# Holding back sixteen DRAM stores in an FFT convolution, and sharing out the evictions behind it

## The chip, the cores and the metric

The kernel runs on one core of a Trainium2 chip. The metric is the device time of one execution, in microseconds. A core has five engines that run beside each other, each through its own instruction stream in order: TensorE (PE in the profile; its weight loads are listed as PEld), VectorE (DVE), ScalarE (ACT), GpSimd (POOL) and SyncE (SP). In this kernel nearly every DMA is issued by SP, so SP's stream is the queue of the transfers: an issue that has to wait holds up all the issues behind it.

## What is computed

Four layers on an array x of 2048 positions by 512 features: local attention, long convolution, local attention, long convolution, each on a layernorm of x and added to it.

```python
x = A_x
x = x + _A_ref(_layernorm(x, axis=-1), A_wqkv, A_wo)
x = x + _B_ref(_layernorm(x, axis=-1), B_A_re, B_A_im, B_B_re, B_B_im, B_C_re, B_C_im, B_log_dt, B_Dskip)
x = x + _A_ref(_layernorm(x, axis=-1), A_wqkv, A_wo)
x = x + _B_ref(_layernorm(x, axis=-1), B_A_re, B_A_im, B_B_re, B_B_im, B_C_re, B_C_im, B_log_dt, B_Dskip)
```

The change lies in the first `_B_ref` (and at the border to the second attention). With the transforms cut to what matters:

```python
K = jnp.einsum("dn,dnl,dn->dl", Cc, P, dB).real      # one convolution kernel per feature
Kf = rfft2(pad(K)); Uf = rfft2(pad(u))
Yf = Uf * Kf
y = irfft2(Yf)[..., :L] + u * Dskip
```

The spectrum Kf is the same in both convolution layers. The first convolution computes it, uses it, and writes it to DRAM; the second reads it back.

## The kernel before

Class `FftB` is one convolution layer; `tag` is 0 for the first and 1 for the second. The features are in two groups (g = 0, 1), and the length-4096 transform is done in two steps of matmuls each way. The order of the work is written out by hand, as a string of tokens that `run` (line 829) walks through; each engine then executes its share in that order. For the first convolution the string is `ORDER0`, and then `ORDERF`, which also carries the beginning of the second attention layer. The tokens:

- `K`, `U`: first transform step of the convolution kernel and of the input (`f1`, line 711): PE, then an eviction from PSUM by DVE (`D`) or ACT (`A`) into the tile a1s.
- `k`: second step of the convolution kernel (`k_f2`, line 730). One token gives one *piece* of the spectrum, 128 partitions by 1024 values of bf16 (256 KB); there are 16 pieces, k0 to k15. The piece is evicted (line 709) into a slot taken from the list `self.free`.
- `u`: second step of the input (`u_f2`, line 776), evicted by ACT into one of three `ub` buffers (line 782).
- `m`: the product of piece n with the input's spectrum (`u_mult`, line 764): two DVE instructions (line 769), the first with the piece itself, `kn`, the second with `ks`, the same piece with each pair of neighbouring partitions exchanged (the other part of a complex product). They add to the tiles t1 and t2 of the group.
- `y`: first step back (`i1`, line 784), y0 to y7 from the t tiles of group 0, y8 to y15 from those of group 1. So y8 can only start when the last product, m15, is done. 32 matmuls and one eviction each.
- `z`: last step back (`i2`, line 801), which adds to x_sb; `z01D` is group 0, row block 1, by DVE.
- In `ORDERF`, `h`, `a`, `p`, `n`, `T`, `E`, `P`, `Q` are the layernorm statistics, the transposes and the K and Q projections of the second attention layer.

The exchanged copy `ks` is made by two DMAs per piece (`kf_load`, line 750, issues at line 755), SBUF to SBUF, 64 partitions (128 KB) each. Here they are called the *exchange* of piece n. `pump` (line 745) issues the exchanges up to four ahead of the products, or further while slots are plentiful; it is called after each `k` and each `m`. After each product the piece is stored to DRAM by one DMA of 256 KB (line 772, the *store* of piece n), and both slots go back to the list. The store only reads `kn`, so it does not wait for the product itself.

Slots: twelve at first, three in the part of the tile w_sb that w2 leaves over (here w0, w1, w2), six in kn tiles (kn0a to kn2b), three in kf_sb (wk0 to wk2); eight more (kf_nat) when the last `K` token is done. In the profile they go by those tile names. Before the change the exchanges and stores around the middle of the stage stand on SP in this order (target <- source):

```
store 0 (w0) | exchange 4 (w0<-kn2b) | store 1 (w2) | exchange 5 (w1<-wk0) | store 2 (kn0b) |
exchange 6 (w2<-wk1) | store 3 (kn1b) | exchange 7 (kn0a<-wk2) | store 4 | exchange 8 (kn1a<-kn0b) |
exchange 9 (kn2a<-kn1b) | store 5 | exchanges 10, 11, 12 | store 6 | exchange 13 | exchange 14 |
store 7 | exchange 15 (w1<-wk0) | stores 8 to 15 | weights of the second attention layer
```

PSUM: `ptile` (line 704) deals out four buffers in turn, so a tile of PSUM is written again four tiles later. In `ORDERF` the last five tiles of group 0 (y3 to y7) are evicted by ACT, y8 by ACT, y9 by DVE, y10 to y12 by ACT, then z01 by DVE, y13 by DVE, y14 and y15 by ACT.

The weights of the second attention layer are loaded by `front_w` (line 226): two DMAs of 512 KB into the tile kT_ext, the half for K first (line 227), the half for Q (line 228). That tile lies over memory that w_sb and the kn tiles held before, so these DMAs wait for the stores that read it. `front_k` (line 255) is the first to use it.

Of the kernel before, what the change touches and what calls it, by code (L numbers as in the profile page):

```python
# [21 lines left out]
S = 2048  # L22
# [15 lines left out]
NG = 2  # L38
DQG = 64
EC = 16  # L40
NEC = 128 // EC
# [12 lines left out]
"""  # L54
LATE0 = "a s t g r b m"
ORDERF = """
yA yA yA yA yA yA yD yA yA yA z01D yD yA yA z00A z10A z11A h01 h00 h10 a0 z12A
p0 h11 z02A n0 a1 z03A h02 S T0 p1 E01D n1 E00A h12 a2 z13A P02 P01 h03 T1
E10A Q00 E11D p2 P03 P00 n2 h13 P10 P12 a3 T2 E21D E20A p3 n3 P11 P13 P23 P21
T3 E31D x1 E30A P20 P22  # L60
"""
ORDER1 = """
UD UA UD UA UD UA UD UA UD UA UD u UD u u m UA u m UD UA m u m u m
# [112 lines left out]
class LayerA:  # L176


    def __init__(self, tc, nc, consts, lnst, A_wqkv, A_wo, layer, xnT, nq):
        self.tc, self.nc, self.c, self.lnst, self.layer = tc, nc, consts, lnst, layer  # L180
        self.ctx = ExitStack()
        self.keep = self.ctx.enter_context(tc.tile_pool(name=f"a{layer}_keep", bufs=1, side="right"))
        slot = self.keep.tile([P, NDT * (2 * D + (NA + 14) * P)], BF16, name="kT_ext", tag="slot")
        self.wqk = slot[:, 0:NDT * 2 * D].rearrange("p (t c) -> p t c", t=NDT)
        self.wsrc = A_wqkv.rearrange("(dt p) c -> p dt c", p=P)
        self.A_wo = A_wo
        self.kT = slot[:, NDT * 2 * D:].rearrange("p (t a q) -> p t a q", t=NDT, q=P)
        self.xnT = xnT
        self.qT = {q: self.q_tile(q) for q in range(nq)}
        self.ps_l = self.wv = None  # L190
        self.xns = {}
        self.st = [dict() for _ in range(4)]
# [477 lines left out]
class FftB:  # L670


    def __init__(self, tc, nc, C, ident, w2_dram, g2_dram, kf_dram, x_sb, tag):
        self.tc, self.nc, self.C, self.ident, self.kf_dram, self.x_sb = tc, nc, C, ident, kf_dram, x_sb
        self.w2_dram, self.g2_dram = w2_dram, g2_dram
        self.tag = tag
        self.c_grp, self.c_mid, self.c_ps = ExitStack(), ExitStack(), ExitStack()
        self.grp = self.c_grp.enter_context(tc.tile_pool(name=f"b{tag}_grp", bufs=5, reuse_waits="tile"))
        self.ps = [c.enter_context(tc.tile_pool(name=f"b{tag}_ps_{side}", bufs=2, space=PSUM, side=side))
                   for c, side in ((self.c_ps, "right"), (self.c_grp, "left"))]  # L680
        self.npt = 0
        self.kf, self.nat, self.ub, self.cnt = {}, {}, {}, {}
        self.nkf = 0
        g2p = self.c_grp.enter_context(tc.tile_pool(name=f"b{tag}_g2", bufs=1, reuse_waits="tile"))
        self.g2 = g2p.tile([P, 2, 16, P], BF16, name="g2_sb")
        self.S = [dict() for _ in range(NG)]
# [43 lines left out]
    def k_f2(self, g, ec, eng):  # L730
        n = g * NEC + ec
        p2 = self.f2(g, "ka", ec)
        kf = self.nat[n] = self.free.pop(0)
        self.evac(kf, p2, eng)
        self.nk += 1
        self.pump()
# [13 lines left out]
    def kf_load(self, n):  # L750
        sync, (g, ec) = self.nc.sync, divmod(n, NEC)
        if self.tag == 0:
            kn, ks = self.nat[n], self.free.pop(0)
            for h in range(2):
                sync.dma_start(ks[h::2], kn[1 - h::2])
            self.kf[n] = kn, ks
            return
        kc = self.ring[n % len(self.ring)]
        sync.dma_start(kc[0::2], self.kf_dram[g, ec])
        for r in range(2):  # L760
            sync.dma_start(kc[1::2, r], self.kf_dram[g, ec, :, 1 - r])
        self.kf[n] = kc[:, 0], kc[:, 1]

    def u_mult(self, g, ec):
        n = g * NEC + ec
        kn, ks = self.kf.pop(n)
        ub = self.ub.pop(n)
        for t, k in zip(self.S[g]["t"], (kn, ks)):
            self.nc.vector.tensor_tensor(t[:, :, ec * EC:(ec + 1) * EC], ub[:], k, ALU.mult)  # L769
        self.nm += 1  # L770
        if self.tag == 0:
            self.nc.sync.dma_start(self.kf_dram[g, ec].rearrange("p r q e -> (p r) (q e)"), kn.rearrange("p q e -> p (q e)"))
            self.free += [kn, ks]
        self.pump()

    def u_f2(self, g, ec):
        nc = self.nc
        if ec == 0:
            self.S[g]["t"] = tuple(self.gtile(n, [P, DQG, P]) for n in ("t1", "t2"))
        p2 = self.f2(g, "ua", ec)  # L780
        ub = self.ub[g * NEC + ec] = self.wk.tile([P, DQG, EC], BF16, name="ub")
        nc.scalar.copy(ub[:], p2)  # L782
# [660 lines left out]
```

## Time and profile before

| | us |
|---|---|
| median of 3 runs | 420.19 (419.57 to 420.63) |
| the profiled execution, as timed | 420.44 |
| its span in the trace | 418.6 |
| DVE busy | 387.1 (92% of the span) |
| ACT busy | 323.0 (77%) |
| PE busy | 321.3 (77%) |
| stores of pieces (line 772) | 16 issues of 256 KB, 3.3 median from issue to landing |
| exchanges (line 755) | 32 issues of 128 KB, 3.4 median to landing |

The profiled execution took 420.44 us, 1.84 more than its span; that is what lies before the first and after the last instruction of the trace. The mean granted clock of TensorE was 0.981 of full speed. The first convolution runs from about 195 us of the span to about 262 us; the products m0 to m15 lie between 213.77 and 243.90.

In the lines of an engine's order of time, the first number is the start in us from the span's start, the second the duration, then engine, source line, operation and tiles (out<-in); in brackets at the end stands how long the engine had been idle, and what released it. "SPq" is SP issuing a DMA. In lines by window the columns are the window and its length, busy time of PE, PEld, DVE, ACT and POOL with the number of instructions in brackets, granted clock, busy share of the DMA engines, and GB/s.

### The profile page before, as it was taken

To read this page: it belongs to the slowest core of one execution; us is meant where nothing else is said; L and a number is where in the kernel's file an instruction comes from. 1 tells how busy PE (TensorE), PEld (TensorE's weight loads), DVE (VectorE), ACT (ScalarE), POOL (GpSimd) and SP (SyncE) were. 2 spreads that over 40 slices of the span, in tenths; PEclk is the share of its full clock that TensorE was granted. 3 is DMA by queue.
4 is the path that set the end of the run, shared out by engine and by line. 5 is a ranking of instruction groups with operands and counts; after the bars stand their busy time and mean duration, and the time that the engine had idled before them with its cause. 6 is when DMAs were issued, how large, how long until landed. Compare 5 with 4: busy or idle time off the path is not lost.

```text
span 418.6 us, 15862 instructions
## 1 busy us (share of the span) xinstructions
PE 321.3 (77%) x7046; PEld 232.5 (56%) x7104; DVE 387.1 (92%) x515; ACT 323.0 (77%) x554; POOL 37.7 (9%) x46
## 2 busy tenths in 40 slices
PE   3000068999999987888998779999998978896785
PEld 2000036667756555556887668556555656666664
DVE  8999999999899999997999949979779999989995
ACT  5999998986445569997999978874555657889972
POOL 3000200000396000001400000000000020000000
PEclk9999998999999999999999969999999998999999
DMA  7940642123015666393245597730043018504506
GB/s 205 390 132 13 73 90 70 33 45 84 15 39 136 171 173 189 85 397 114 78 146 199 187 307 207 208 121 2 2 115 89 3 56 351 155 3 131 176 7 199
DMA packets 62462, 54.36 MB, mean 130 GB/s; under 512 B 33877, under 2 KB 50874, under 8 KB 61114
## 3 DMA queue, kind: packets, MB, share of 16 engines
q1 hardware_dynamic: 62250, 53.22, 42.1%
q8 instruction: 55, 0.90, 0.9%
q10 hardware_dynamic: 144, 0.13, 0.1%
q14 instruction: 13, 0.11, 0.1%
HBM read 30.28 MB, written 13.24 MB: 104 GB/s over the span
## 4 chain that ended last, share of the span: by engine, by line
PE 38%; DVE 24%; ACT 9%; DMA 7%; issue 6%; SPq 1%; DVEq 0%; ACTq 0%
DVE pav L413 8%; PE pq L359 6%; DVE a1s L709 4%; PE L L315 4%; DVE t L769 4%; PE pk L1139 4%; PE po L428 4%; PE pq L439 3%; PE pq L198 3%; DVE prod L308 3%; PE pp L255 3%; PE pp L1077 3%; DMA w_sb<-w_dram 2%; PE pb L796 2%; PE pb L821 1%
## 5 line engine op out<-in xcount | busy, mean ns | idle before, releaser
L413 DVE TENSOR_TENSOR pav<-attn,v_ext 128x4096 bf16<-128x4096 bf16 (+1 forms) x34 | 72.9, 2158 | 0.2 <-PE pq L439 0.2
L308 DVE TENSOR_TENSOR prod<-qT,kT_ext 128x4096 bf16<-128x4096 bf16 x29 | 66.0, 2300 | 3.9 <-PE L L315 3.8
L428 PE MATMUL po<-ident,pav 64*128 64x64 bf16 x2048 | 36.7, 192 | 14.2 <-DVE pav L413 8.1
L428 PEld LDWEIGHTS <-pav 64*128 64x128 bf16 x2048 | 33.2, 96 | 25.0 <-DVE pav L413 15.6
L1067 PE MATMUL pt<-ident,x_blk 128*128 128x128 bf16 x64 | 7.0, 260 | 43.4 <-ACT x_blk L171 43.4
L979 DVE TENSOR_TENSOR A_t<-A_t,pow_t 128x1024 bf16<-128x1024 bf16 (+4 forms) x46 | 38.1, 870 | 0.2
L439 PE MATMUL pq<-wop,oT 128*128 128x512 bf16 x121 | 31.6, 380 | 4.0 <-issue 3.6
L782 ACT CAST ub<-pb 128x1024 bf16<-128x1024 f32 x32 | 32.2, 1035 | 1.8 <-DVE t L769 0.8
L361 ACT CAST v_ext<-pq 128x512 bf16<-128x512 f32 x32 | 18.8, 587 | 19.2 <-PE pq L359 17.5
L727 PE MATMUL pb<-a1s,w_sb 128*128 128x64 bf16 x768 | 27.2, 193 | 6.4 <-ACT a1s L709 2.9
L315 PEld LDWEIGHTS <-prod 128*128 128x128 bf16 x928 | 27.0, 96 | 8.1 <-DVE prod L308 2.5
L1067 PEld LDWEIGHTS <-x_blk 128*128 128x128 bf16 x64 | 5.4, 117 | 46.1 <-ACT x_blk L171 44.3
L359 PE MATMUL pq<-wv,xnT 128*128 128x512 bf16 x118 | 29.9, 379 | 0.5
L709 DVE CAST a1s<-pb 128x1024 bf16<-128x1024 f32 x23 | 27.0, 1216 | 3.4 <-PE pb L720 3.4
L1077 PE MATMUL pp<-xnT,kT_ext 128*128 128x512 bf16 x87 | 24.9, 404 | 6.4 <-ACT qT L1082 3.4
L727 PEld LDWEIGHTS <-w_sb 128*128 128x128 bf16 x768 | 24.8, 98 | 8.7 <-issue 6.9
L315 PE MATMUL L<-ind,prod 128*128 128x8 bf16 x928 | 27.4, 166 | 0.8 <-DVE prod L308 0.6
L430 ACT CAST oT<-po 128x512 bf16<-128x512 f32 x32 | 18.5, 577 | 11.8 <-PE po L428 11.6
L709 ACT CAST a1s<-pb 128x1024 bf16<-128x1024 f32 x25 | 24.9, 1034 | 2.2 <-PE pb L720 1.9
L796 PE MATMUL pb<-Wp,t 64*128 64x64 bf16 x512 | 20.5, 198 | 5.9 <-ACT ub L782 3.4
L796 PEld LDWEIGHTS <-t 64*128 64x128 bf16 x1024 | 18.7, 100 | 11.0 <-issue 6.5
L1139 PEld LDWEIGHTS <-A_t 128*64 128x64 bf16 (+1 forms) x512 | 22.2, 105 | 3.6
(225 smaller groups left out, 818.9 us busy)
## 6 DMA issues: line engine op xcount, KB each, us to landing
w_sb<-w_dram SPq DMA_DIRECT2D x8, 1024.0 KB, 9.7
w_dram<-w_zero SPq DMA_DIRECT2D x1, 4096.0 KB, 14.7
kf_ring<-kf_dram SPq DMA_DIRECT2D x13, 256.0 KB, 3.9
kf_ring<-kf_dram SPq DMA_DIRECT2D x26, 128.0 KB, 4.0
v_ext<-v_ext SPq DMA_DIRECT2D x4, 784.0 KB, 6.0
x_blk<-in_A_x_dram SPq DMA_DIRECT2D x4, 512.0 KB, 4.2
kT_ext<-in_A_wqkv_dram SPq DMA_DIRECT2D x4, 512.0 KB, 10.2
x_sb<-in_A_x_dram SPq DMA_DIRECT2D x4, 512.0 KB, 5.8
```

Of the source, the lines that this page charges most:

```text
L308: nc.vector.tensor_tensor(pr, self.qT[q][:, ft].unsqueeze(1).to_broadcast([P, W, 4, P]), kap, ALU.mult)
L315: self.nc.tensor.matmul(L[:, al, w, ft * 8:(ft + 1) * 8], lhsT=pr[:, w, al, :], rhs=self.c["ind8"][:], start=(ft == 0 and w == 0 and al % ...
L359: nc.tensor.matmul(pp[:], lhsT=xnT[:, dt, a * P:(a + 1) * P], rhs=wv[:, dt, :], start=(dt == 0), stop=(dt == NDT - 1))
L413: nc.vector.tensor_tensor(pv[:, i], attn[:, n % 4].unsqueeze(2).to_broadcast([P, W, DH // parts, H]), vap, ALU.mult)
L428: nc.tensor.matmul(po[:, h, 0, i * nt + ft, :], lhsT=pvf[rows, i, w, ft * P:(ft + 1) * P], rhs=ident[rows, rows], start=(w == 0 and ft + i ...
L439: nc.tensor.matmul(pw[:], lhsT=oT[:, ftp, :], rhs=self.wo[:, ftp, :], start=False, stop=(ftp == NDT - 1))
L709: (self.nc.scalar.copy if eng == "act" else self.nc.vector.tensor_copy)(dst, src)
L727: nc.tensor.matmul(p2[:, j, :], lhsT=self.w2[:, ec * EC + j, :], rhs=a1s[:, ec * EC + j, :], start=True, stop=True)
L796: nc.tensor.matmul(p3[:, h, j, :], lhsT=tt[rows, dql, :], rhs=w[rows].rearrange("p m d -> p (m d)"), start=first, stop=not first)
L979: return lambda: nc.vector.tensor_tensor(*args)
L1077: nc.tensor.matmul(pps[kind, b, ft][:], lhsT=la.wqk[:, dt, c:c + P], rhs=la.xnT[:, dt, b * 512:(b + 1) * 512], start=(dt == 0), stop=(dt = ...
L1139: nc.tensor.matmul(o, lhsT=lhs, rhs=Bt[:, ri, c * CH + ql].rearrange("p b g -> p (b g)"), start=(not half and j % 4 == 0 and ri == 0), sto ...
```

## The change

Two things are changed.

**Stores.** After a product in the first convolution the piece is put on a list, `held`, and only `ks` goes back to the free slots; then `pump` issues exchanges; then, for the first four products, or once all sixteen exchanges are issued, everything held is stored, and the slot of each stored piece becomes free. If a slot is wanted and none is free, the oldest held piece is stored first (`slot`). Each exchange still stands at the same token as before. On SP the order becomes:

```
exchange 4 (w1<-kn2b) | store 0 (w0) | exchange 5 (w0<-wk0) | store 1 (w2) | exchange 6 (kn0a<-wk1) |
store 2 (kn0b) | exchange 7 (w2<-wk2) | store 3 (kn1b) | exchange 8 (kn0b<-kn1a) |
exchange 9 (kn1b<-kn2a) | exchanges 10, 11, 12, 13 | exchange 14 (w0<-w1) | exchange 15 (w2<-kn0a) |
stores 4 to 15 | weights of the second attention layer
```

**Evictions.** At the head of `ORDERF`, y3 to y15 are evicted A A A D A D A D A D, z01D, A D A instead of A A A A A A D A A A, z01D, D A A.

```diff
 ORDERF = """
-yA yA yA yA yA yA yD yA yA yA z01D yD yA yA z00A z10A z11A h01 h00 h10 a0 z12A
...
+yA yA yA yD yA yD yA yD yA yD z01D yA yD yA z00A z10A z11A h01 h00 h10 a0 z12A p0 h11 z02A n0 a1
...
+        self.held = []
...
     def k_f2(self, g, ec, eng):
-        kf = self.nat[n] = self.free.pop(0)
+        kf = self.nat[n] = self.slot()
...
     def kf_load(self, n):
-            kn, ks = self.nat[n], self.free.pop(0)
+            kn, ks = self.nat[n], self.slot()
...
     def u_mult(self, g, ec):
...
         if self.tag == 0:
-            self.nc.sync.dma_start(self.kf_dram[g, ec].rearrange("p r q e -> (p r) (q e)"), kn.rearrange("p q e -> p (q e)"))
-            self.free += [kn, ks]
+            self.held.append((g, ec, kn))
+            self.free.append(ks)
         self.pump()
+        if self.tag == 0 and (self.nm <= 4 or self.nkf == NG * NEC):
+            while self.held:
+                self.kf_store()
+
+    def kf_store(self):
+        g, ec, kn = self.held.pop(0)
+        self.nc.sync.dma_start(self.kf_dram[g, ec].rearrange("p r q e -> (p r) (q e)"), kn.rearrange("p q e -> p (q e)"))
+        self.free.append(kn)
+
+    def slot(self):
+        if not self.free:
+            self.kf_store()
+        return self.free.pop(0)
```

The rest of `ORDERF` is the same tokens in the same order.

More of the change, by code (lines that the diff above doesn't have):

```diff
@@ L56 @@
 ORDERF = """
-yA yA yA yA yA yA yD yA yA yA z01D yD yA yA z00A z10A z11A h01 h00 h10 a0 z12A
-p0 h11 z02A n0 a1 z03A h02 S T0 p1 E01D n1 E00A h12 a2 z13A P02 P01 h03 T1
-E10A Q00 E11D p2 P03 P00 n2 h13 P10 P12 a3 T2 E21D E20A p3 n3 P11 P13 P23 P21
-T3 E31D x1 E30A P20 P22
+yA yA yA yD yA yD yA yD yA yD z01D yA yD yA z00A z10A z11A h01 h00 h10 a0 z12A p0 h11 z02A n0 a1
+z03A h02 S T0 p1 E01D n1 E00A h12 a2 z13A P02 P01 h03 T1 E10A Q00 E11D p2 P03 P00 n2 h13 P10 P12
+a3 T2 E21D E20A p3 n3 P11 P13 P23 P21 T3 E31D x1 E30A P20 P22
 """
```

## The prediction

> **What bounds the kernel now.** I read the chain of waits first, around the products of the first convolution, then the order of time of DVE, SP and ACT there, then granted clock and busy times by window. The chain:
>
> ```profile
> 213.77 1.30 DVE t L769 x2
> 215.89 4.21 DMA kf_dram<-w_sb
> 221.33 3.40 DMA kf_dram<-kn
> 239.29 3.83 DMA w_sb<-kf_sb
> 243.21 0.70 DVE t L769
> 243.96 4.39 PE pb L796 x158
> ```
>
> Two stores (1 and 3) and the exchange of piece 15 stand in it, then m15, then PE with y8. What these transfers really cost is seen on DVE:
>
> ```profile
> 224.85 1.23 DVE L709 CAST kn<-pb 128x1024 bf16<-128x1024 f32 x1 [0.45 <-DMA kf_dram<-kn]
> 241.42 0.69 DVE L769 TENSOR_TENSOR t<-ub,kf_sb 128x1024 bf16<-128x1024 bf16 x1
> 243.21 0.69 DVE L769 TENSOR_TENSOR t<-ub,w_sb 128x1024 bf16<-128x1024 bf16 x1 [1.10 <-DMA w_sb<-kf_sb]
> ```
>
> DVE waits 0.45 us for store 3, which still holds the slot k9 is evicted into, and 1.10 us for the exchange of piece 15. These are its only waits from 203.57 to 243.90, so DVE sets the pace of the products, and the transfers cost 1.55 us in all. Why the last exchange is late is told by SP:
>
> ```profile
> 220.18 1.10 SPq L755 DMA_DIRECT2D w_sb<-kf_sb  x2
> 221.33 1.50 SPq L772 DMA_DIRECT2D kf_dram<-kn  x1
> 226.10 1.10 SPq L755 DMA_DIRECT2D kn<-kn  x2
> 235.86 2.19 SPq L755 DMA_DIRECT2D w_sb<-kn  x2
> 238.10 0.58 SPq L772 DMA_DIRECT2D kf_dram<-kf_sb  x1
> ```
>
> ACT had evicted piece 15 at 232.43, but its exchange is issued at 238.78, behind stores 4 to 7 and the other exchanges. A half of an exchange takes SP about 0.57 us (1.10 for two) and a store 0.59, but now and then an issue takes one more microsecond or so (the 1.50 and the 2.19 above, 1.81 at 232.12); from 214 to 241 there are six such among the issues of stores 1 to 9, while the eight halves at 203.42 to 210.47 have none. Last, the clock:
>
> ```profile
> 239.17:242.58 3.41, 2.03 (x98) 1.57 (x95) 2.94 (x5) 3.37 (x4) 0.00 (x0) 1.00 0.63 231
> 242.58:246.00 3.42, 2.04 (x78) 2.04 (x80) 0.85 (x2) 3.24 (x4) 0.35 (x1) 0.50 0.97 361
> 246.00:249.41 3.41, 3.41 (x96) 3.01 (x91) 1.06 (x1) 2.72 (x3) 0.00 (x0) 0.50 0.98 295
> 249.41:252.82 3.41, 3.41 (x113) 2.91 (x112) 2.92 (x4) 2.00 (x3) 0.00 (x0) 1.00 1.10 366
> ```
>
> PE has nothing from about 242.2 until m15 is done at 243.90. Its granted clock is halved at 242.58 and stays so for two windows of 3.41 us, while PE is the one busy engine: in the third line PE is busy for all of it, DVE for a third.
>
> **The change, part by part.** *The waits removed.* k9 now goes into kn2a, the `ks` of m3, which DVE itself has read by 224.4: the 0.45 go. Exchange 15 no longer has stores 4 to 7 ahead of it. If it is in time, the 1.10 go too, and m15 ends at 243.90 - 1.55 = 242.35.
>
> *The waits added.* The target of exchange 5 is now w0, the piece stored by store 0; exchange 7 waits so for store 1, exchange 8 for store 2, exchange 9 for store 3. And store 0, out by 211.09 before, comes behind exchange 4, which has to wait for the second instruction of m0 (its end 215.05, plus the 0.29 that SP took after the first one: 215.34). Each store is followed through with a landing of 3.40 (store 3 in the chain) or 4.21 (store 1), and with 1.15 from an exchange's start to the store behind it (214.74 to 215.89):
>
> - store 0 at 216.49, landed 219.9 to 220.7; exchange 5 then, store 1 at 221.1 to 221.9, landed 224.5 to 226.1;
> - exchange 6 right behind, store 2 at 223.0 to 223.8, landed 226.4 to 228.0;
> - exchange 7 at 224.6 to 226.2 (behind it in SP's queue are all the later exchanges), store 3 at 225.8 to 227.4, landed 229.2 to 231.6;
> - exchange 8 at 226.5 to 228.1, exchange 9 at 229.2 to 231.6, against 226.10 before.
>
> So exchange 9 is some four microseconds later; call its time T. Its second half is issued at T + 0.52 and lands 2.1 to 3.4 later (median of the halves with an empty queue at 203 to 206, and of those around 226). m9 needs it at 233.22 (233.67 before, less 0.45). With T in the middle, 230.3, and 2.7 to land, it is there at 233.5: about 0.3 late, which I take as nothing lost beyond the rounding. After m9, m15 ends 8.4 later by DVE's own work (234.36 for m9 to 243.90, less the wait of 1.10): the wait pays until T = 231.6, where 231.6 + 0.52 + 2.7 + 0.69 + 8.4 = 243.9, the old end.
>
> Exchanges 10 to 15 then follow without a store between: the second half of 15 starts at T + 1.2 + 11 x 0.57 = 237.8, or 240.1 if two of the long issues still fall among them. It was 239.29. Landing 2.1 to 3.8 later (3.83 in the chain), it is there at 239.9 to 243.9, against 241.66, when DVE comes to it; from the side of the first I take it as in time, because the eight halves without stores had no long issue. Sum so far, m15: -1.55, bounds -1.55 and about +0.9 (T = 231.6 plus a late piece 15), more if stores land slower.
>
> *The stretch behind m15.* From 243.90 to 252.90 PE does y8 to y12, z01, y13 to y15 and z00 without a pause worth naming. At half clock a y took 4.39/5 = 0.88; at full clock 96 matmuls, three y, took 1.51 (249.87), 0.50 each; z01 took 1.51 at half clock, z00 1.53 at full. All at full clock: 8 x 0.50 + 0.9 + 1.53 = 6.4 instead of 9.0. Then the evictions set the pace: 1.22 on DVE and about 0.95 on ACT, one PSUM tile in four. With the new turns, DVE has y6, y8, y10, y12, z01 (from m15 on, 1.15 each), ACT y7, y9, y11: y12's tile waits for y8's eviction, z00 ends some 6.9 after m15. With the old turns ACT was busy with y3 to y7 until 244.80 and would hold it to about 8.5. So this edit is worth nothing at half clock (ACT waited 0.69 for PE at 246.69) and up to 1.6 at full: it is there to cash in what the clock gives. DVE can carry the three evictions more: it was busy for 5.0 of the 10 us from 244 to 254. The clock: the two other drops in this trace (65.09 to 68.50 and 344.98 to 348.39) lasted one window, and there PE was busy for 3.17 and 3.06 us of it; here it was busy for 2.04, since it began 1.4 us into it. With y8 at 242.4 the window to 246.00 is full. I take one half-clock window: 3.41 us give 3.9 y, the rest 1.1 x 0.50 + 0.9 + 1.5 + 1.53 = 4.5, together 7.9, a gain of 1.1; bounds 0 (two windows again) and 2.1 (none).
>
> The Trainium skill ("TensorE: Matmul & The Clock Gate", section "Why this matters for your kernels") asks only that gaps of more than about 3 us be avoided, since it takes an idle window to lose the clock. This gap was 1.7 us and the clock fell within 0.4 us of its start, so the row stands against the rule. By the rule the gap would not be the cause, closing it would not help, and the sum would end at -1.55.
>
> *What moved behind.* Stores 4 to 15, twelve in place of eight, now end SP's stage: at 0.72 each (eight took 5.78 from 239.94) from 238.4 the last starts at 246.3 and, with the 4.9 of before, lands at 251.2. The K weights (line 227) wait for it: issued about 251.3, 245.89 before; with 7.2 to land, 258.5. PE first uses them at 262.0, then 2.65 earlier, at 259.4: 0.9 of cover. Gone, it would cost what it is late by. The Q half comes 0.6 later, used at 264.6. The loads behind these (wv, wop) are used from about 288 on and have tens of us.
>
> Sum: -0.45 - 1.10 - 1.1 = -2.65. The profiled execution took 420.44 (418.6 and 1.84 around it), so 417.8; the median of the runs is 0.25 below it, so I expect **417.5**. The attention layer behind is a closed chain of PE, DVE and ACT work, with no transfer that comes at a fixed time, so nothing swallows the gain there.
>
> **Rivals.** (a) *Only the two waits fall*: the clock drops for two windows all the same, for the window's position is not the kernel's to set. For it: the busy time of PE before the drop (2.03 of 3.41) hardly changes; against it: windows with as little kept the clock (2.05 from 157.25 on). 420.19 - 1.55 = 418.6. (b) *The wait moves from exchange 15 to exchange 9*: T about 231.6, m15 where it was. For it: stores did land in 4.2 us with little else in flight; against: 3.3 is their median. 420.2. (c) *Slower: the store round trips ahead of exchange 9.* Decides from T = 231.6 on. If stores 0, 1 and 3 land in 4.9 each, the longest seen here, T is 231.6 + 3 x 0.7 = 233.7, m15 ends 2.1 later than before, the clock is lost for two windows as before, and the time is 420.19 + 2.1 = 422.3. For it: all exchanges stand in one queue behind that wait; against: 4.9 was seen with eight stores queued.
>
> **How the numbers follow.** Chances: forecast 0.40, (a) 0.20, (b) 0.22, (c) 0.18. Three runs before spread over 1.06 us, so 0.3% (1.26 us) is about what a measurement can tell from no change: faster is below 418.93, slower above 421.45. Faster takes nearly all of the forecast and most of (a): 0.54; same the rest of (a), (b) and a little of (c): 0.27; slower 0.19. The forecast's own range is 416.5 (both bounds good: 1.55 + 2.1) to 418.6; with the spread of the runs, and reaching over (b) and the milder part of (c): 415.9 to 421.3.
>
> **What would show it.** Right: no DVE wait at k9 and at m15, exchange 15 issued before 238.5, y8 beginning near 242.4, the half clock at most one window long, SP waiting on stores 0, 1 and 3 for 2 to 4 us each. Wrong: DVE idle before the second instruction of m9, with exchange 9 after 231.6; PE idle before y8 as long as before; PE waiting at line 255 for the K weights.

## The result, and the profile after

The changed kernel is slower: 421.81 us median of 22 runs (418.84 to 423.23), against 420.21 us of 22 runs of the kernel before on the same chip (418.12 to 422.81). The ratio is 1.0038, 95% interval 1.0021 to 1.0054, or 1.6 us (0.9 to 2.3). The prediction was 417.5 us, range 415.9 to 421.3. Ratios and means leave out the few executions that took over 1.5% more than the fastest one of their kernel.

The profiled execution took 420.79 us, with a span of 419.0 (before: 420.44 and 418.6). It misleads: the stage that the change touches went *faster* in it. First the order of time of DVE around the products:

```profile
226.04 1.21 DVE L709 CAST kn<-pb 128x1024 bf16<-128x1024 f32 x1
236.59 4.89 DVE L769 TENSOR_TENSOR t<-ub,kf_nat 128x1024 bf16<-128x1024 bf16 x8
243.21 0.68 DVE L769 TENSOR_TENSOR t<-ub,w_sb 128x1024 bf16<-128x1024 bf16 x1
```

k9 and m15 have no bracket of idle time any more, so the 0.45 and the 1.10 are gone. From m0 to the end of m15 it takes 28.39 us here (215.50 to 243.89), and took 30.14 before. SP in order of time:

```profile
220.97 1.11 SPq L755 DMA_DIRECT2D w_sb<-kf_sb  x2
225.69 1.10 SPq L755 DMA_DIRECT2D w_sb<-kf_sb  x2
227.59 2.97 SPq L755 DMA_DIRECT2D kn<-kn  x4
230.66 6.32 SPq L755 DMA_DIRECT2D kf_nat<-kf_nat  x8
238.37 2.07 SPq L755 DMA_DIRECT2D w_sb<-kn  x2
252.46 0.39 SPq L226 DMA_DIRECT2D kT_ext<-in_A_wqkv_dram  x1
```

Lines 1 and 2 are exchanges 5 and 7, which wait for stores 0 and 1. Line 3 holds exchanges 8 and 9; 9 starts at 229.45, which is 13.96 after m0 (12.33 before). Line 4 is exchanges 10 to 13, eight halves in 6.32 us; line 5 is exchange 15, 22.87 after m0 (25.01 before). The K weights follow at 252.46. Then the windows behind m15, with the columns as in the prediction (busy PE, PEld, DVE, ACT, POOL, then the granted clock):

```profile
242.98:246.40 3.42, 2.63 (x144) 2.33 (x144) 3.42 (x5) 3.18 (x5) 0.00 (x0) 1.00 0.86 321
246.40:249.81 3.41, 1.98 (x70) 1.55 (x64) 3.15 (x3) 0.93 (x1) 0.00 (x0) 1.00 1.02 377
249.81:253.22 3.41, 3.41 (x90) 3.12 (x90) 2.54 (x5) 2.77 (x3) 0.35 (x1) 1.00 0.25 87
```

The clock was not halved at all in this stretch, which was the best case of the prediction. Still the second of these windows holds only 1.98 us of matmuls. The chain of waits says what PE did there (start, length, what):

```profile
245.08 1.77 PE pb L809 x96
247.83 0.51 PE pb L809 x28
248.34 1.43 issue
249.78 1.17 PE pb L809 x68
```

"issue" is time in which PE waited for nothing that the profile shows. Here it stopped 1.43 us in the middle of its work, in a stretch at full clock. So although no window was at half clock, m15 to the first layernorm row of the second attention (xn, line 172) took 14.02 us; with two such windows it had taken 14.62. Lastly the end of the program, the last eviction of the kernel before and then of the changed one:

```profile
413.60 0.59 ACT L827 CAST x_sb<-pb 128x512 bf16<-128x512 f32 x1 [0.95 <-PE pb L822]
```

```profile
413.45 0.59 ACT L840 CAST x_sb<-pb 128x512 bf16<-128x512 f32 x1 [0.95 <-PE pb L835]
```

From its start to the end of the span it is about 5.0 us before (418.6) and about 5.5 us after (419.0).

### The profile page after: what moved, and what is told of

It is laid out like the page before. It is cut to its first block, busy times and chain, and to the rows that moved or that the text cites. A ratio compares the mean times of both kernels' runs of the same rounds, so it can differ in the third digit from the quotient of the medians.

```text
span 419.0 us, 15919 instructions
## 1 busy us (share of the span) xinstructions
PE 328.1 (78%) x7104; PEld 232.6 (56%) x7104; DVE 390.4 (93%) x518; ACT 320.4 (76%) x551; POOL 37.8 (9%) x46
## 4 chain that ended last, share of the span: by engine, by line
PE 44%; DVE 21%; ACT 9%; issue 5%; DMA 3%; SPq 2%; DVEq 0%; ACTq 0%
DVE pav L412 7%; PE pq L358 6%; PE pk L1152 5%; DVE t L769 4%; PE L L314 4%; DVE a1s L709 4%; PE pp L1090 4%; PE po L427 4%; PE pq L197 4%; PE pp L254 3%; PE pq L438 3%; PE pb L809 2%; SPq L1257 2%; ACT ub L795 2%; PE pb L727 1%
## 5 line engine op out<-in xcount | busy, mean ns | idle before, releaser
L727 PE MATMUL pb<-a1s,w_sb 128*128 128x64 bf16 x768 | 28.9, 197 | 6.8 <-ACT a1s L709 2.9
L438 PE MATMUL pq<-wop,oT 128*128 128x512 bf16 x128 | 34.2, 391 | 0.0
L727 PEld LDWEIGHTS <-w_sb 128*128 128x128 bf16 x768 | 26.2, 100 | 9.3 <-issue 7.4
L1090 PE MATMUL pp<-xnT,kT_ext 128*128 128x512 bf16 x96 | 26.2, 401 | 6.0 <-ACT qT L1095 3.1
L1152 PE MATMUL pk<-B_t,A_t 128*64 128x84 bf16 (+1 forms) x512 | 23.6, 201 | 0.0
```

What stands on the lines that cost most here:

```text
L438: nc.tensor.matmul(pw[:], lhsT=oT[:, ftp, :], rhs=self.wo[:, ftp, :], start=False, stop=(ftp == NDT - 1))
L727: nc.tensor.matmul(p2[:, j, :], lhsT=self.w2[:, ec * EC + j, :], rhs=a1s[:, ec * EC + j, :], start=True, stop=True)
L1090: nc.tensor.matmul(pps[kind, b, ft][:], lhsT=la.wqk[:, dt, c:c + P], rhs=la.xnT[:, dt, b * 512:(b + 1) * 512], start=(dt == 0), stop=(dt = ...
L1152: nc.tensor.matmul(o, lhsT=lhs, rhs=Bt[:, ri, c * CH + ql].rearrange("p b g -> p (b g)"), start=(not half and j % 4 == 0 and ri == 0), sto ...
```

## The experiments

There were twelve runs in three groups, each group beside its own runs of the kernel before. The theories that the expectations name:

- **R**, round trips: exchanges 5, 7, 8 and 9 wait in SP's one queue for stores 0 to 3, and everything behind them comes late.
- **S**, stores: twelve stores in a burst at the end of the stage cost time by their traffic or by delaying the K weights.
- **E**, evictions: the new turns cost, or gain, something themselves.
- **C**, clock: only the windows at half clock fall differently.

The table has the stages of every trace, each time counted from the start of m0 (us), and the ratio to the kernel before. "Half clock" counts, in windows of 3.41 us, the drop of the clock that reaches into the stretch from m15 to xn. The four rows with "one run" repeat a kernel without an edit: the kernel before, the changed kernel (twice) and the kernel with the first four stores early.

| kernel | exchange 9 | exchange 15 | end of m15 | m15 to xn | half clock | ratio (95%) |
|---|---|---|---|---|---|---|
| before | 12.33 | 25.01 | 30.14 | 14.62 | 2 | 1 |
| before again | 12.24 | 24.55 | 29.66 | 13.72 | 1 | one run |
| turns only | 12.24 | 24.90 | 30.16 | 14.24 | 2 | 1.0018 (0.9987 to 1.005) |
| stores on GpSimd | 12.24 | 24.87 | 29.86 | 15.88 | 1 | 1.0022 (0.9993 to 1.0052) |
| after | 13.96 | 22.87 | 28.39 | 14.02 | 0 | 1.0038 (1.0021 to 1.0054) |
| after again | 15.98 | 25.94 | 30.99 | 14.08 | 2 | one run |
| after, third | 16.26 | 25.90 | 30.49 | 13.75 | 1 | one run |
| stores only | 16.73 | 26.85 | 32.24 | 14.43 | 2 | 1.0053 (1.0026 to 1.0081) |
| first two early | 12.37 | 22.48 | 28.40 | 14.38 | 0 | 1.0003 (0.9977 to 1.0028) |
| first four early | 12.24 | 22.15 | 28.77 | 13.54 | 1 | 0.9984 (0.9955 to 1.0012) |
| first four early again | 12.88 | 22.63 | 29.49 | 14.07 | 0 | one run |
| first four early, old turns | 12.24 | 21.69 | 28.40 | 13.84 | 0 | 1.0024 (0.9998 to 1.0049) |
| no round trips | 12.24 | 22.30 | 28.40 | 14.10 | 1 | 0.9991 (0.9958 to 1.0025) |
| exchange on two queues | 12.73 | 19.08 | 29.34 | 13.75 | 0 | 0.9994 (0.997 to 1.0017) |

### The two parts alone

Stores only: the change with the old head of `ORDERF`.

```diff
-yA yA yA yD yA yD yA yD yA yD z01D yA yD yA z00A ...
+yA yA yA yA yA yA yD yA yA yA z01D yD yA yA z00A ...
```

> The stores held back, the evictions of y3 to y15 as before. Theory S (the stores cost it: twelve of them now stand together ahead of the second layer's weights, and their traffic falls on what comes after): this kernel is as slow as the changed one, ratio to before about 1.004. Theory E (the evictions cost it: VectorE takes three more of them): ratio at or below 1.000, since the products then still end about 1.7 us earlier after m0. Theory C (neither costs anything by itself; the products and the stretch behind them are shorter by about 2.6 us as in the one profile after, and the loss is windows of half clock that fall elsewhere): m0 to m15 about 27.7 us against 29.4 in the profile, total anywhere from 0.997 to 1.004, with the difference to before outside the stage.

Measured: 422.57 us, ratio 1.0053 (1.0026 to 1.0081). The loss comes with the stores, so E falls; R and S both allow this. DVE in this trace shows where:

```profile
234.54 0.69 DVE L770 TENSOR_TENSOR t<-ub,kn 128x1024 bf16<-128x1024 bf16 x1 [1.63 <-DMA kn<-kn]
238.57 3.10 DVE L770 TENSOR_TENSOR t<-ub,kf_nat 128x1024 bf16<-128x1024 bf16 x5 [0.40 <-DMA kf_nat<-kf_nat]
245.02 0.69 DVE L770 TENSOR_TENSOR t<-ub,w_sb 128x1024 bf16<-128x1024 bf16 x1 [1.55 <-DMA w_sb<-kn]
```

The first line is the second instruction of m9, waiting 1.63 us for exchange 9: the very place that rival (c) named. It is followed by two more waits, 3.58 us in all, where the kernel before waits 1.55. m15 ends 32.24 after m0.

Turns only: the kernel before (each store at once after its product) with the new head of `ORDERF`.

```diff
-yA yA yA yA yA yA yD yA yA yA z01D yD yA yA z00A ...
+yA yA yA yD yA yD yA yD yA yD z01D yA yD yA z00A ...
```

> The evictions in turn, stores as before. Theory S: ratio 0.998 to 1.000, the stage behind m15 no longer than before. Theory E: ratio about 1.004, with a longer stretch from m15 to the first transposes of the second attention layer than in before (15.3 us from the second instruction of m15 to the first layernorm output). Theory C: 1.000 with the products unchanged from before.

Measured: 420.87 us, ratio 1.0018 (0.9987 to 1.005): no difference that can be told. DVE waits 1.52 us at m15, as before. Its profiled span of 422.7 is no verdict: m0 began at 217.72 there, 3.95 later than before, in code that both share.

### The round trips taken away

First four early: stores 0 to 3 are issued ahead of the slots' release and of `pump`, as in the kernel before; all others are held. The burst at the end stays.

```diff
             self.held.append((g, ec, kn))
+            if n < 4:
+                self.kf_store()
             self.free.append(ks)
```

> The changed kernel, but stores 0 to 3 are issued ahead of the exchanges as before; stores 4 to 15 stay held back. Tells whether the round trips of stores 0 to 3 cost anything: if they do, exchange 9 is issued some 2 us sooner after m0 than the 13.95 us of the changed kernel, and the time falls by up to 1 us against it. Theory S (the cost is in the late end of the stores) and theory C: exchange 9 sooner, products no faster, ratio to before still about 1.004 (S) or within 0.997 to 1.004 (C).

Measured: 420.07 us, ratio 0.9984 (0.9955 to 1.0012). SP in order of time:

```profile
222.42 0.58 SPq L783 DMA_DIRECT2D kf_dram<-kn  x1
226.07 2.38 SPq L755 DMA_DIRECT2D kn<-kn  x4
228.57 7.23 SPq L755 DMA_DIRECT2D kf_nat<-kf_nat  x8
237.19 1.73 SPq L755 DMA_DIRECT2D kn<-w_sb  x2
250.81 0.39 SPq L226 DMA_DIRECT2D kT_ext<-in_A_wqkv_dram  x1
```

Exchange 9 (third and fourth issue of line 2) is back at 12.24 after m0, DVE waits only 0.28 us (at k9), and the change's loss is gone (I had expected a microsecond of it back at most). The stores still end late and the K weights still come 35.77 after m0, against 32.12 before. S would have kept the loss at about 1.004, so S falls as the main cause; the upper end of the interval, 1.0012, leaves room for half a microsecond.

No round trips: stores 0 to 3 are not issued here at all, their slots are free at once, and four extra stores of pieces 12 to 15 go into the places of pieces 0 to 3, so the burst is longer. The second convolution then reads four wrong pieces; the amount of work is the same.

```diff
-            self.held.append((g, ec, kn))
-            self.free.append(ks)
+            if n >= 4:
+                self.held.append((g, ec, kn))
+            if n >= 12:
+                self.held.append((0, ec - 4, kn))
+            self.free += [ks, kn] if n < 4 else [ks]
...
-        self.free.append(kn)
+        if g or ec > 3:
+            self.free.append(kn)
```

> The changed kernel without stores 0 to 3 among the exchanges: their slots are free at once, and four stores are issued at the end of the stage instead, which write pieces 12 to 15 into the places of pieces 0 to 3 (so the second convolution reads four wrong pieces; as many stores and bytes as ever, sixteen exchanges in one row). Theory R (the round trips of stores 0 to 3, which exchanges 5, 7, 8 and 9 wait for, cost the changed kernel 1.5 to 4 us in most executions): m0 to m15 at most 28.8 us in the profile, no wait of VectorE at m9, total 0.993 to 0.998 of before. Theory S (the late end of the stores costs it): the stores end later still, total at or above that of the changed kernel, 1.004 or more. Theory C (only the windows of half clock move): 0.997 to 1.004, products of 28 to 29 us in both.

Measured: 419.08 us, ratio 0.9991 (0.9958 to 1.0025); no wait on DVE, 28.40 to the end of m15, although the last store starts 34.35 after m0. The ratio is above the 0.993 to 0.998 that R gave and below S's 1.004: with the round trips the loss is gone, but nothing clear is gained over the kernel before.

First two early: half of the round trips.

```diff
             self.held.append((g, ec, kn))
+            if n < 2:
+                self.kf_store()
             self.free.append(ks)
```

> The changed kernel with stores 0 and 1 alone issued at once; the exchanges that write over the pieces of stores 2 and 3 still wait for them. Half of the round trips. Theory R, with each round trip worth its part: exchange 9 starts 13 to 14.5 after m0 (12.24 with none, 13.96 to 16.73 with four), m0 to the end of m15 in 28.4 to 30, ratio 0.998 to 1.003. Theory S (the late end of the stores and their traffic costs, whenever the first four go): 1.003 to 1.005 as in the changed kernel.

Measured: 419.46 us, ratio 1.0003 (0.9977 to 1.0028), with exchange 9 at 12.37 and no wait on DVE. So the four do not cost a part each, as I had it. Here store 3 is issued 8.45 after m0 and has landed at 12.30, which is hardly later than piece 9 can go anyway (exchange 8 has to wait for piece 8, evicted at 11.02, and 12.24 is the earliest exchange 9 of all traces). The two round trips that are left fit into this slack; with all four, store 3 is issued at 11.34 to 12.42.

### The spread of one kernel

The kernel before and the changed one, unaltered:

> The kernel before once more, for a second execution in detail. All theories: m0 to m15 within 1 us of the 30.14 of the first one; the span may differ by up to 2.5 us with the windows of half clock ahead of m0.

Measured: span 420.1, with 0.96 us of waiting at m15, and 29.66 to its end.

> The changed kernel once more, for a second execution in detail. Theory R: m0 to m15 is spread, near the 32.2 of the kernel with the stores alone more often than near the 28.4 of the first one, and wherever it is long VectorE waits at m9 or behind for an exchange, with exchange 9 more than 14 us after m0. Theory C: 28.4 again, within half a us.

Measured: span 419.2. SP and then DVE in order of time:

```profile
226.64 4.31 SPq L755 DMA_DIRECT2D kn<-kn  x4
231.05 7.36 SPq L755 DMA_DIRECT2D kf_nat<-kf_nat  x8
239.80 2.20 SPq L755 DMA_DIRECT2D w_sb<-kn  x2
```

```profile
238.96 1.89 DVE L769 TENSOR_TENSOR t<-ub,kf_nat 128x1024 bf16<-128x1024 bf16 x3 [0.92 <-DMA kf_nat<-kf_nat]
242.95 0.69 DVE L769 TENSOR_TENSOR t<-ub,w_sb 128x1024 bf16<-128x1024 bf16 x1 [1.49 <-DMA w_sb<-w_sb]
```

The same code as in the profile after, yet exchange 9 is 2.02 us later against m0, eight halves take 7.36 instead of 6.32, DVE waits 2.41 us, and m15 ends at 30.99 instead of 28.39. Theory C, which had 28.4 again, falls as the whole account.

> The changed kernel once more, for its spread. Theory R: m0 to the end of m15 between 28.4 and 32.3 and exchange 9 between 14 and 17 after m0, the two moving together. If instead the products take 28.4 with exchange 9 at 16 or later, R falls.

Measured: span 420.8, exchange 9 at 16.26, waits of 0.90 (m9) and 1.01 (m15), m15 at 30.49. Both lie where R has them, though they do not move strictly together: after again had 15.98 with 30.99.

> The changed kernel with stores 0 to 3 issued at once, once more. Theory R: exchange 9 at 12.2 to 12.5 after m0 and m0 to the end of m15 in 28.3 to 29.2, as in the first such run (12.24 and 28.77): with no round trip there is no spread. If it takes 30 or more, the spread is not from the round trips.

Measured: span 420.4, exchange 9 at 12.88 and 29.49 to the end of m15, both a little above what I gave. The excess is one wait, 1.00 us at k9 for store 3, which still holds k9's slot in this version. So the spread without the round trips is not nil: 28.40 to 29.49 over the six traces with early or no stores 0 to 3 (or 0 and 1), against 28.39 to 32.24 over the four with the round trips.

### Is it SP's queue?

Stores on GpSimd: the old places of the stores and the new turns, with the stores issued by POOL.

```diff
-            self.nc.sync.dma_start(self.kf_dram[g, ec]..., kn...)
+            self.nc.gpsimd.dma_start(self.kf_dram[g, ec]..., kn...)
```

> Stores at their old places, but issued by GpSimd, whose queue is empty in this stage, and the evictions in turn. Exchanges then have no store ahead of them in SP's queue, and the stores end no later than the products. Theory S: the gain of the stage (about 2.6 us) stays and the cost goes: ratio 0.994 to 0.997. Theory E: about 1.000. Theory C: anywhere from 0.993 to 1.001, products of about 27.7 us.

Measured: 421.54 us, ratio 1.0022 (0.9993 to 1.0052). With no store left on SP, exchange 15 still starts 24.87 after m0, and m15 waits 1.37 us. SP in order of time, exchanges 10 to 13:

```profile
229.24 7.65 SPq L754 DMA_DIRECT2D kf_nat<-kf_nat  x8
```

From exchange 9 to exchange 15 it takes 12.63 us, as in the kernel before (12.68), which has three stores in between; six of SP's twelve issues there last more than 1 us, three of fifteen before. With the stores held back the same stretch takes 8.9 to 10.1, with one or two such issues. So to take the stores off SP's queue did not help while they were issued among the exchanges all the same. Whether their transfers slow SP's issues, or the issuing by POOL does, no run tells. As the exchanges were no earlier, the run is no test of S either.

Exchange on two queues: the first four early, and the second half of each exchange issued by POOL.

```diff
-            for h in range(2):
-                sync.dma_start(ks[h::2], kn[1 - h::2])
+            for h, q in enumerate((sync, self.nc.gpsimd)):
+                q.dma_start(ks[h::2], kn[1 - h::2])
```

> The kernel with stores 0 to 3 early and the rest held back, and the second half of every exchange issued by GpSimd instead of SP. If the issue rate of the one queue is what makes piece 15 late (0.88 us per half in the stretch of six exchanges), the last exchange is issued about 5 us sooner after m0 and the products run without a wait, 28.4 us or less; total 0.994 to 0.997 of before. If the transfers themselves are the limit, the last exchange lands no sooner and the total stays at the 0.998 of the kernel it is made from.

Measured: 419.92 us, ratio 0.9994 (0.997 to 1.0017). Exchange 15 comes 19.08 after m0, three microseconds earlier than with one queue (I had expected five), so the pace of the one queue did hold it back. Nothing is gained: once DVE does not wait for it, how early it is no longer matters. DVE's one wait left is 0.85 at k9, for store 3.

### The turns once more

First four early, with the old turns:

> Stores 0 to 3 issued at once as in the run of the first four stores early, and the evictions with their old turns. Only the evictions differ from that run. Theory E (the new turns cost, or gain, something themselves): the ratio to the kernel before moves from 0.998 by 0.3% or more, to 1.001 if they gain 1.2 us and to 0.995 if they cost as much; the time from the end of m15 to the first transpose of the second attention layer (13.54 with the new turns) moves by a microsecond or more. Theory R (the round trips of stores 0 to 3 are what the change loses on, the turns are worth nothing): 0.997 to 1.000, that stretch 13.3 to 14.5, and m0 to the end of m15 in 28.4 to 29.2.

Measured: 420.62 us, ratio 1.0024 (0.9998 to 1.0049), against 0.9984 (0.9955 to 1.0012) with the new turns in another group. The ratio stands where theory E put a gain of the turns, while the stretch that the turns act on, 13.84, stands where R had it. Over the three pairs that differ in the turns alone, new against old, the ratios move by +0.18% (before and turns only), -0.15% (stores only and after) and -0.40% (this pair): both signs, the first two well within their intervals, the third just at the edge of what two such intervals allow. I leave it at no effect shown; up to some 0.4% either way is not excluded. All twelve held stores were in this kernel too, so its upper end also leaves room for a small cost of the burst. From the kernel with the stores alone (1.0053, 1.0026 to 1.0081) it differs by the round trips only, and there the intervals overlap: the case for R rests on all five versions without the four round trips, not on this pair.

## Why the prediction was wrong, point by point

**The waits removed: right.** With the stores held back, wherever exchange 9 was not late, the wait at m15 went. Four traces have no wait on DVE at all from m0 to m15, and there it takes 28.39 to 28.40, which is 30.14 less 1.55 and a little. The -1.55 was there to be had.

**The round trips: place right, the time of exchange 9 in part by luck.** I put exchange 9 at 230.3, that is 16.5 after m0, in a range of 15.4 to 17.8; the four traces have 13.96, 15.98, 16.26 and 16.73. SP waits for stores 0 and 1 (2.3 to 3.0 us together) and for store 3 (0.7 to 1.15); I had given 2 to 4 each, too much. Long issues that the sum did not have (1.5 to 2.1 us, at exchanges 6 and 8 in the three late traces) made up for it. In all four, exchange 9 goes out within 0.1 us of the landing of store 3. That store took 3.9 to 4.5 us to land in the late traces and 2.54 in the profile after: this is the lucky end of the spread.

**The step that failed** is the one behind it: "Exchanges 10 to 15 then follow without a store between", at 0.57 us a half, "because the eight halves without stores had no long issue". By it the first half of exchange 15 starts at T + 1.2 + 10 x 0.57 = T + 6.9 (T + 9.2 with the two long issues that I took as the worse case). Measured it is T + 8.9, 10.0, 9.6 and 10.1. It takes 9.5 to 10.1 in the versions on one queue with early or no stores 0 to 3 as well, where also no store stands between. Of the twelve issues in this stretch ten or eleven are short, 0.55 to 0.56 us in the mean, about as forecast. What the term left out is most of 1.26 us of pauses between the issues, the same in all four traces, and one or two long issues, which together take 1.1 to 2.2 us more than short ones would. So the long issues do not belong to the stores. And the eight halves that I took the pace from were no unbroken row:

```profile
205.96 4.50 SPq L755 DMA_DIRECT2D kn<-kn  x4
```

These are the last four of them: 4.50 us for 2.2 us of issues, because SP stood from 207.21 to 209.36 waiting for piece 3 to be evicted. With 9.9 (the mean of the three late traces) in place of 6.9, exchange 15 at T = 16.5 comes at 26.4 after m0, and the 25.01 of the kernel before is reached at T = 15.1, not at the 17.8 (231.6) that I gave as break-even. The traces agree: 13.96 wins, 15.98 and later lose. In all three late traces the wait that ends last is at m14 or m15, for exchange 14 or 15. The waits at m9 in two of them come before it and have another source: the second half of exchange 9 landed 3.48 and 3.74 after its issue, where I took 2.7. So "I take it as in time" for exchange 15, and with it "nothing lost", was wrong from the middle of my own range of T.

Rival (c), slower by the round trips ahead of exchange 9, had the round trips and the wait at m9, and a price (422.3) near the measured time, but let m9 decide. By exchange 15 the point of decision is 2.7 us earlier, so its chance of 0.18 was too small.

**The stretch behind m15: -1.1 forecast, nothing found.** Over the four traces with the round trips it took 13.75 to 14.43 us, in the three of before's stores on SP 13.72 to 14.62. It does not follow the clock: with no window at half clock it took 13.75 to 14.38, with one 13.54 to 14.10 (stores on GpSimd aside), with two 14.08 to 14.62. My sum for full clock had PE running through, and PE did not. The kernel with the first two stores early, also at full clock, has the same stop in its chain:

```profile
245.42 0.22 PE pb L836
246.40 0.51 PE pb L811 x28
246.92 1.54 issue
248.46 1.17 PE pb L811 x68
```

The place in the program is the same as in the profile after, 28 matmuls into the y that follows z01, and first four early again stops there for 1.48. What stops PE there is not shown by a run. The trace has a transfer of 16 KB on the queue of kind "instruction" just ahead of it (247.44 to 248.32 in the profile after, 246.00 to 246.88 here), while the burst of stores fills the DMA engines (busy share 1.02 in the windows above); PE waiting for its own code fits, and is argued only. With the first four early and the old turns there is no such stop, but ACT's evictions follow on each other without a pause there and set the pace.

The Trainium skill ("TensorE: Matmul & The Clock Gate", section "Why this matters for your kernels") is concerned with gaps of more than about 3 us. Here the clock was halved without one. In seven traces PE has a gap of 1.4 to 2.0 us ahead of y8 (1.59 in the kernel before, where I read 1.7) and the clock drops near it, but in two of them (after again, stores only) before the gap begins. In two more (first four early, no round trips) it drops with no gap above 0.6. The stops of 1.0 to 1.5 us in four traces, and one of 2.37 with the stores on GpSimd, left it whole. So to keep to that rule is not enough in this stretch, and my reading of the row, that this gap sets the clock, is not borne out.

**The evictions: worth nothing, as said** for the half clock. The 1.6 at full clock did not show: at full clock m15 to xn took 13.75 to 14.38 with the new turns and 13.84 in the one trace with the old.

**The K weights: no cost, as forecast.** Forecast 37.5 after m0, measured 36.97 in the profile after and 39.33 to 40.36 in the three others. Both halves had landed 2.7 to 4.2 us before PE's first use of them (line 254, or 255 in stores only), so the cover held.

**The size of the loss.** Means of the four traces with the round trips against the three of before's stores on SP: m0 to m15 30.53 against 29.99, +0.5; m15 to xn 14.07 against 14.19, -0.1; the end of the program +0.45. Together +0.85, with the measured interval 0.9 to 2.3. So few traces, with 3.9 us between the fastest and the slowest products, do not pin the rest down. Part of it may lie in the clock. The mean granted clock of a whole execution is 0.982 both in the changed kernel (20 executions) and with the stores alone (11), 0.986 to 0.987 in the kernel before (68 in the three groups of experiments) and 0.984 to 0.989 in all other versions; executions below 0.95 are left out. Within one kernel 0.001 less clock went with 0.1 to 0.3 us more time (0.19 in a fit over all of them), so the 0.0045 that is missing goes with some 0.8 us, by estimate. Where these windows fall, and whether the late products bring them on, the four traces do not show. The end of the program is 5.45 to 5.49 us after the last addition to x_sb begins in the eight traces of the versions that hold stores back (those on two queues and without round trips left aside), 5.00 to 5.07 in the two traces of the kernel before and in those of turns only and no round trips, and 4.65 in the two in which POOL issues DMAs. It is the one part that does not scatter. The difference lies behind the landing of the last output: from there to the end it takes 1.51 to 1.54 us in the kernel before and the two like it and 1.95 to 1.99 in the eight. Its cause is open.

**Better than both?** Not shown. Without the four round trips the ratios are 0.9984, 0.9991, 0.9994 and 1.0003, and 1.0024 with the old turns, all with 1 inside the interval: some 1.2 us fewer in the products (28.80 in the mean of six traces against 29.99), of which the end of the program gives 0.45 back.

## What to carry to other kernels

A wait that is put ahead of the last transfers in a queue costs by the pace of what is queued behind it: take that pace from the stretch itself, long issues and all, and not from the best stretch in the trace. Holding a buffer's store back lets other transfers pass, and turns every transfer that reuses the buffer into one that waits for a full store; ask for each held buffer who wants it next. One profile of a stage that hangs on such a chain can show its lucky end: here the profiled execution was 1.75 us faster in the stage in a kernel that is 1.6 us slower.

## What the runs showed of the hardware

- SP's issue of a half of an exchange takes 0.46 to 0.61 us in nearly all cases, with one of 1.0 to 2.3 us in between, in most stretches every 4 to 6 us. The kernel before has transfers of the instruction queue at 231.94, 236.25 and 240.56, and long issues on SP at 232.12 (1.81), 236.45 (1.61) and 240.57 (1.71); in the profile after, 233.60 and 238.10 against 234.09 (1.61) and 238.37 (1.43), while the one at 229.03 falls into SP's wait ahead of exchange 9, as the one at 207.32 in the kernel before falls into its wait among the eight halves. In the thirteen traces other than the one with the stores on GpSimd, all 69 issues of exchanges and stores on SP that last more than 1 us overlap a transfer of this queue; with the stores on GpSimd, three of the six between exchanges 9 and 15 do not. So they go together, but not always, and that one makes the other was not tried.

```profile
q8 instruction: 55, 0.90, 0.9%
```

That is the queue's line in the profile after: packets, MB, share of the 16 engines. It looks like nothing, and its packets of 16 KB stand beside the long issues that the prediction left out.

- Windows at half clock fall differently in each execution of the same code: they begin at 65.09, 242.58 (two) and 344.98 in the first trace of the kernel before and at 158.64, 247.39 and 346.38 in the second. The stage moves too: m0 began at 213.77 and 216.50 in these two, and at 215.50, 213.86 and 215.53 in the three traces of the changed kernel. A stage has to be compared from a mark of its own, not from the span's start.
